# Two half-size DMAs for each streamed weight half, P.V of quad 6 inside Q of quad 7, and V's stores issued by SyncE

## The chip, the core and the metric

The kernel runs on one core of one Trainium2 chip. Its engines work side by side, each on its own stream of instructions: TensorE (PE, matmuls; PEld is its weight loads), VectorE (DVE), ScalarE (ACT), GpSimd (POOL) and SyncE (SP), which here only issues DMAs. Sixteen DMA engines move the data. The metric is the device time of one execution in microseconds; less is better.

## What is computed

Four layers in a row on a sequence of 2048 tokens of width 640: A, B, A, B, each on a layer-normed input with a residual. A is attention with a recurrent memory: the sequence is cut into 64 segments of 32 tokens, 8 memory rows stand ahead of each, and what comes out in the memory rows is the memory of the next segment. B is a dilated sliding-window attention (8 keys, 2 apart). Cut to what matters here:

```python
def _A_ref(x, mem0, Wq, Wk, Wv, Wo, seg_len):      # 32 heads of 192
    for s in range(n_seg):                         # 64 segments of 32 tokens
        h = concatenate([mem, xs])                 # 8 + 32 rows of 640
        q, k, v = h @ Wq, h @ Wk, h @ Wv           # each 640 x 6144
        p = softmax(where(mask, q @ k.T * scale, -1e9))
        o = (p @ v) @ Wo                           # 6144 x 640
        mem = o[:, :M]
        outs.append(o[:, M:])
...
x = x + _A_ref(_layernorm(x), ...)
x = x + _B_ref(_layernorm(x), ...)
x = x + _A_ref(_layernorm(x), ...)
x = x + _B_ref(_layernorm(x), ...)
```

## The kernel before

**Two lanes.** The memory makes the segments of a layer follow each other, but the second pair of layers needs only segments that the first pair has finished. So step `t` computes segment `t` of the first A layer and segment `t - 2` of the second A layer together, as two lanes of 40 rows: a matmul has 128 x 128 weights and 80 moving columns. The B layers of the segments one step back are mixed in. There are 66 steps with A and a last one with B alone; the first two and the last two have one lane (`one_lane`).

**Quads.** The 32 heads are taken four at a time, as eight quads. For quad `i` a step makes K (`a_k`), Q (`a_q`) and V (`a_v`), 30 matmuls each, in `proj`; the scores (`a_s`, eight matmuls), their exponential on ScalarE and the mask on VectorE (`a_mask`); P.V (`a_pv`, eight matmuls) and, on ScalarE behind it, the reciprocal of the sums `R` (four logarithms and an exponential); the product of P.V and `R` on VectorE (`a_norm`); and the output projection (`a_o`, 30 matmuls), which runs several quads late. P.V of quad `i - 1` stands in the iteration of quad `i`. `step` writes the order of all engines out by hand; nothing reorders it. After quad 6's iteration it goes on: K of quad 7, P.V of quad 6, Q of quad 7, output of quad 2, norm of quad 6, scores of quad 7, mask of quad 7, output of quad 3, P.V of quad 7, and then outputs of the quads that are left, the layer norm of the next step among them. `a_vt` does nothing there in a step of two lanes.

**Weights.** A's weights are 32 units (k, q, v, o by eight quads), each of two halves of 128 x 1920 bf16, 480 KB. 40 of the 64 halves stay in SBUF. The other 24 are read again in every step through a ring of four buffers (`wring`, tile `w_ring`). `prefetch` runs down a list of loads and issues those that have a free buffer; `used` is called where the last matmul that reads a half has been written and hands its buffer back, so that the DMA of the next half waits for that matmul. In `proj`, `used` for the first half is called before the 16th matmul. All weight loads are issued by SyncE, in order: what waits there holds up what stands behind it.

A streamed half lies in memory as two contiguous blocks of 128 x 960 (`PIECE`), the first for columns 0 to 959 of every partition and the second for the rest; one DMA reads both (line 264), in 256 packets of 1920 bytes. A matmul of K, Q or V reads 128 columns out of chunk `c` (384 columns each) of a half; one of the output projection, 128 columns out of row block `m` (640 columns each).

**V through memory.** For quads 2 to 7 in steps of two lanes V is transposed without TensorE: VectorE transposes 32 x 32 blocks (`v_blocks`, into `vB`), `v_send` stores them to DRAM (`v_rows`, 144 KB, 128 packets, six times a step), and `v_fetch` reads them back in another order into `Vt` (120 KB, six times a step), which P.V reads. `v_send` is issued by ScalarE's queue and `v_fetch` by SyncE's. `v_send` of quads 2 to 4 stands behind `v_fetch` of the quad before, at the end of an iteration; that of quads 5, 6 and 7 stands right behind Q of quads 3, 4 and 5.

**Completions.** Every DMA adds to one of eight completion semaphores, which the program hands out in turn over all DMAs; a DMA that takes a semaphore waits until the DMA that had it eight earlier has landed.

Of the kernel before, what the change touches and what calls it, by code (L numbers as in the profile page):

```python
# [17 lines left out]
P = 128  # L18
# [14 lines left out]
PIECE = 960  # L33
# [12 lines left out]
HALF = 1920  # L46
# [41 lines left out]
def pair_in_one(resident, kind, i):  # L88

    return all((kind, i, h) in resident for h in range(2)) and (kind, i) != ("o", NQUAD - 1)  # L90

class Kernel:
# [142 lines left out]
    def prefetch(self):  # L235

        while self.loads:
            key = self.loads[0]
            kind, i, h = key
            n = 1  # L240
            if kind == "b":
                if any(self.kept_uses[u] < 2 for u in self.under(i)):
                    return
                self.loads.pop(0)
                self.load_b_weights(i)
                continue
            if self.n_loaded < N_HALVES and key in self.kept:
                at = self.kept_at[key]
                t_ = self.wb[:, at:at + HALF]
            elif key in self.resident:  # L250
                n += pair_in_one(self.resident, kind, i)
                t_ = self.wres.tile([P, n * HALF], BF16, name="w_%s%d%d" % key)
            elif self.ring_free:
                t_ = self.wring.tile([P, HALF], BF16, name="w_ring")
                self.ring_free -= 1
            else:
                return
            del self.loads[:n]
            self.n_loaded += n
            src = self.wsrc[kind][i, P * HALF * h:P * HALF * (h + n)]  # L260
            if key in self.resident:
                self.nc.sync.dma_start(out=t_[:, 0:n * HALF], in_=src.rearrange("(p c) -> p c", p=P))
            else:
                self.nc.sync.dma_start(out=t_[:, 0:HALF].rearrange("p (a c) -> p a c", c=PIECE), in_=src.rearrange("(a p c) -> p a c", p=P, c=PIECE))
            for j in range(n):
                self.units[kind, i, h + j] = t_[:, j * HALF:(j + 1) * HALF].rearrange("p (a b) -> p a b", a=3 if kind == "o" else NC)

# [30 lines left out]

        return self.acc[int(c >= 3)], c - 3 * int(c >= 3)

    def proj(self, kind, i, t):

        nc = self.nc
        hT = self.hT
        ps = self.big(f"ps_{kind}", {"k": 0, "q": 1, "v": 2}[kind])
        w = [self.units[kind, i, h] for h in range(2)]
        mem_last = (kind, i) == (("k", 0) if self.one_lane() else ("v", VLAG))
        order = [(n, c) for c in range(NC) for n in range(6)] if mem_last else [(n, c) for n in range(6) for c in range(NC)]
        for n, c in order:
            if n == 3 and c == 0 and not mem_last:  # L310
                self.used(kind, i, (0,))
            nc.tensor.matmul(ps[:, NT * n + self.c0:NT * n + self.c1], lhsT=w[n // 3][:, c, P * (n % 3):P * (n % 3 + 1)],  # L312
                             rhs=hT[:, NT * c + self.c0:NT * c + self.c1],
                             start=(c == 0 and (n == 0 or not mem_last)), stop=(c == NC - 1), skip_group_check=mem_last)
        self.used(kind, i, (0, 1) if mem_last else (1,))
        return ps
# [8 lines left out]
        nc.scalar.copy(out=kz[0:64, :, 0, :], in_=pv[0:64, :, 1, :])  # L325
        nc.scalar.copy(out=kz[64:P, :, 1, :], in_=pv[64:P, :, 1, :])

    def a_q(self, i, t):
        ps = self.proj("q", i, t)
        qt = self.ap1.tile([P, 6, NT], BF16, name="QT")  # L330
        self.nc.vector.tensor_copy(out=self.cols(qt[:]), in_=self.cols(ps[:, 0:6 * NT].rearrange("p (a n) -> p a n", a=6)))  # L331
        self.qt = qt
# [56 lines left out]
    def v_send(self, i):  # L389

        self.v_sent[i] = self.vdp.tile([P, 3 * DH], BF16, name="v_rows")
        self.nc.scalar.dma_start(out=self.v_sent[i][:], in_=self.vB[i % 2][:])

    def v_fetch(self, i):

# [368 lines left out]
    def b_alone(self, b):  # L764
# [36 lines left out]
        scaled = lambda dst, src: nc.vector.tensor_tensor(out=dst, in0=src, in1=over_c(r), op=ALU.mult)  # L801
        qb = self.bp.tile([P, 6, NX], BF16, name="QB")[:, 0:NC, on]
        scaled(qb, proj(0, "ps_bq", 0))
        kp = proj(1, "ps_bk", 1)
        vp = proj(2, "ps_bv", 2)
        n = BG * SEG
# [59 lines left out]
    def step(self, t):  # L866
        T = self.n_seg + LAG
        self.set_lanes(t)
        b = t - 1 if t >= 1 else None
        nt = t + 1  # L870
        if t == T:
            return self.b_alone(b)
        ahead = not self.one_lane()
        if ahead:
            self.a_v(VLAG, t)
        for i in range(NQUAD - 1):
            self.a_k(i, t)
            if i >= 1:
                self.a_vt(i - 1)
            if b is not None and i == 1:  # L880
                self.b_ln_apply(b)
            if b is not None and i == 3:
                self.b_mask(b, 1)
            self.a_q(i, t)
            if ahead and 3 <= i <= 5:
                self.v_send(i + 2)
            if ahead and i in V_EARLY:
                self.a_v(V_EARLY[i], t)
            if b is not None and i == 0:
                self.bterms = self.ln_terms(self.nc.vector, self.bsums)  # L890
            if b is not None:
                self.b_first(b, i)
            if i >= 1:
                self.a_pv(i - 1)
            if b is not None and i == 6 and self.one_lane():
                self.b_ot()
            if not ahead:
                self.a_v(i, t)
            if b is not None:
                self.b_second(b, i)  # L900
            if ahead and i in V_LATE:
                self.a_v(V_LATE[i], t)
            if i >= OLAG:
                self.a_o(i - OLAG)
            if b is not None and i == 5:
                self.b_pv(1)
                self.b_norm(1)
            if i >= 1:
                self.a_norm(i - 1)
            self.a_s()  # L910
            if b is not None and i == 0:
                self.b_ln(b)
            self.a_mask()
            if ahead and V_LATE.get(i, 0) > VLAG:
                self.v_blocks(V_LATE[i])
            if ahead and i >= 1:
                self.v_fetch(i + 1)
            if ahead and i <= 2:
                self.v_send(i + 2)
            if b is not None and i == 0:  # L920
                self.b_ln_rstd()
            if b is not None and 2 <= i <= 3:
                self.b_s(2 * i - 3)
            if b is not None and i == 6:
                self.b_wo(b)
            if b in (0, LAG) and i == 6:
                self.band_block(self.maskB[0], 1, 0, int(b == LAG))
            if i == 1:
                if nt < self.n_seg:
                    self.x_load(nt)  # L930
                yseg = t - 2 - LAG
                if yseg >= 0 and yseg % 2 == 1:
                    self.y_store(yseg // 2)
        self.a_k(7, t)
        self.a_vt(6)
        if ahead:
            self.a_pv(6)
        self.a_q(7, t)
        if nt < T:
            self.ln1_sums(nt)  # L940
        if not ahead:
            self.a_pv(6)
            self.a_v(7, t)
        self.a_o(7 - OLAG)
        self.a_norm(6)
        self.a_s()
        self.a_vt(7)
        self.a_mask()
        self.a_o(8 - OLAG)
        if ahead:  # L950
            self.a_pv(7)
        self.a_o(9 - OLAG, slice(0, None if ahead else NC), ahead)
        if nt < T:
            self.ln1(nt)
        if not ahead:
            self.a_pv(7)
        if nt < T:
            self.ln1_rstd()
        self.a_norm(7)
        if not ahead:  # L960
            self.a_o(9 - OLAG, slice(NC, None))
        for i in range(10 - OLAG, 7):
            if t == 0:
                self.warm(16)
            self.a_o(i)
        if nt < T:
            self.ln1_apply(nt)
        if t == 0:
            order = [(m, c) for m in (0, 2, 1) for c in range(NC)] + [(m, c) for cs in ((0, 1, 2), (3, 4)) for m in (3, 5, 4) for c in cs]
            self.warm(8)  # L970
            self.a_o(7, slice(0, 3 * NC), False, order)
            self.warm(16)
            self.a_o(7, slice(3 * NC, None), True, order)
        else:
            self.a_o(7)
        if nt < T:
            self.mem_out(t)
        self.b_x1(t)
# [93 lines left out]
```

## Time and profile before

| | us |
|---|---|
| median of 3 runs | 3284.24 |
| the runs | 3281.96, 3284.24, 3290.99 |
| the profiled execution | 3288.64 |
| its span, first to last instruction | 3286.9 |

The profile is of one execution. Its page gives, for each engine, busy time, share of the span and number of instructions; the granted clock of TensorE (mean 0.988); the DMA queues with packets, bytes and the time that the packets took as a share of sixteen engines over the span; and the chain of work that ended last, with its shares. A view of waits lists, for each engine and line, what ended its idle time: "PE ps_q L312 <- issue: 17.8, 24, 1.9" reads as 17.8 us of TensorE's idle time ahead of line 312's matmuls into `ps_q`, in 24 pieces, the longest 1.9 us. "issue" there means that nothing which the profile shows had been waited for. A timeline lists instructions by time; start and length in us, equal ones merged with their count, and in brackets the idle time ahead and what ended it. Matmuls overlap, so the length of a merged group holds the drain of its last one. q1 is the queue of SyncE's DMAs and q10 that of ScalarE's; q8 and q14 carry instructions.

A step takes about 50 us (3286.9 us for 66 steps and a last short one).

### The profile page before, as it was taken

How to read it: one execution, taken by the hardware profiler on the slowest of the kernel's cores; microseconds unless marked ns; L12 is line 12 of the kernel's file. 1: busy time of each engine (PE TensorE's matmuls, PEld its weight loads, DVE VectorE, ACT ScalarE, POOL GpSimd, SP SyncE). 2: the span in 40 equal slices, each digit the busy share in tenths (PEclk: the TensorE clock that was granted, in tenths of full speed). 3: DMA queues.
4: the chain of work that ended last, by engine and by line, in shares of the span. 5: the costliest groups of instructions: out<-in, count | busy, mean ns of one | idle time of the engine just before them, and what ended most of it. 6: DMA issues, size and time to landing. Idle time of an engine off the chain costs nothing.

```text
span 3286.9 us, 182417 instructions
## 1 busy us (share of the span) xinstructions
PE 3060.5 (93%) x81222; PEld 2957.4 (90%) x81222; DVE 2376.9 (72%) x6010; ACT 1837.4 (56%) x5612; POOL 562.9 (17%) x1024
## 2 busy tenths in 40 slices
PE   6999999999999999999999999999999999999998
PEld 4899999999999999989999999899999999999987
DVE  3677777777777777777777777777777777777775
ACT  2456555555555556556556556556556556556554
POOL 2111111111111111111111111111112111111121
PEclk7999999999999999999999999999999999999999
DMA  9889888888888889888888888888889889888886
GB/s 378 287 278 284 285 279 275 283 274 282 277 273 277 285 262 288 278 260 283 281 267 281 283 268 285 273 273 282 273 271 283 277 281 284 282 272 286 287 276 210
DMA packets 628694, 917.18 MB, mean 279 GB/s; under 512 B 166720, under 2 KB 622912, under 8 KB 627904
## 3 DMA queue, kind: packets, MB, share of 16 engines
q1 hardware_dynamic: 560656, 845.43, 80.7%
q10 hardware_dynamic: 67248, 60.09, 5.6%
q8 instruction: 634, 10.39, 1.3%
q14 instruction: 156, 1.28, 0.1%
HBM read 847.88 MB, written 57.48 MB: 275 GB/s over the span
## 4 chain that ended last, share of the span: by engine, by line
PE 76%; ACT 7%; DMA 6%; DVE 6%; issue 5%; ACTq 0%; SPq 0%
PE ps_v L312 15%; PE ps_q L312 15%; PE ps_acc L459 14%; PE ps_k L312 13%; PE ps_o L428 4%; ACT R L432 4%; PE ps_s L407 2%; PE ps_bs L625 2%; PE ps_s L408 2%; PE ps_bk L573 1%; DMA w_ring<-in_A_Wq_dram 1%; ACT R L434 1%; PE ps_bq L573 1%; PE ps_bv L573 1%; PE ps_vt L374 1%
## 5 line engine op out<-in xcount | busy, mean ns | idle before, releaser
L432 ACT ACTIVATE R<-ps_o 64x160 f32<-64x160 f32 (+1 forms) x2112 | 622.2, 295 | 369.0 <-PE ps_o L428 242.2
L312 PEld LDWEIGHTS <-w_ring 128*128 128x128 bf16 x17550 | 717.9, 100 | 62.5 <-issue 27.3
L610 POOL TENSOR_TENSOR QX<-QB,hmask 128x448 bf16<-128x448 bf16 (+2 forms) x325 | 310.9, 965 | 1506.8 <-ACT QB L588 1085.1
L459 PE MATMUL ps_acc<-OT,w_o 128*128 128x80 bf16 (+1 forms) x9900 | 500.0, 200 | 17.9 <-issue 15.4
L324 ACT CAST KF<-ps_k 128x320 bf16<-128x320 f32 (+1 forms) x528 | 218.5, 414 | 495.6 <-PE ps_k L312 443.4
L312 PE MATMUL ps_v<-hT,w_v 128*128 128x80 bf16 (+1 forms) x10350 | 485.2, 202 | 10.4 <-issue 9.4
L312 PE MATMUL ps_q<-hT,w_q 128*128 128x80 bf16 (+1 forms) x10890 | 475.7, 201 | 19.5 <-issue 9.6
L331 DVE CAST QT<-ps_q 128x480 bf16<-128x480 f32 (+1 forms) x528 | 336.3, 637 | 165.7 <-PE ps_q L312 156.2
L312 PEld LDWEIGHTS <-w_q 128*128 128x128 bf16 x10890 | 426.9, 100 | 28.6 <-issue 20.4
L363 DVE CAST vT<-ps_v 128x480 bf16<-128x480 f32 (+1 forms) x504 | 327.9, 651 | 162.3 <-PE ps_v L312 158.4
L312 PEld LDWEIGHTS <-w_v 128*128 128x128 bf16 x10350 | 421.9, 100 | 13.1 <-issue 11.2
L459 PEld LDWEIGHTS <-w_o 128*128 128x128 bf16 x9900 | 409.4, 100 | 23.6 <-issue 20.6
L442 DVE TENSOR_TENSOR OT<-ps_o,R 128x320 bf16<-128x320 f32 (+1 forms) x528 | 252.6, 478 | 223.0 <-ACT R L434 215.4
L312 PE MATMUL ps_k<-hT,w_k 128*128 128x80 bf16 (+1 forms) x7920 | 351.6, 201 | 20.2 <-issue 16.2
L312 PE MATMUL ps_k<-hT,w_ring 128*128 128x80 bf16 (+1 forms) x7860 | 346.9, 201 | 16.2 <-issue 8.1
L459 PE MATMUL ps_acc<-OT,w_ring 128*128 128x80 bf16 (+1 forms) x5940 | 343.5, 201 | 17.0 <-issue 12.6
L410 ACT ACTIVATE E<-ps_s 80x320 bf16<-80x320 f32 (+1 forms) x528 | 220.0, 417 | 238.4 <-PE ps_s L408 231.5
L312 PEld LDWEIGHTS <-w_k 128*128 128x128 bf16 x7920 | 309.2, 100 | 27.3 <-issue 21.0
L387 DVE STREAM_TRANSPOSE vB<-vT 128x576 bf16<-128x576 bf16 x372 | 287.5, 773 | 6.4
L459 PEld LDWEIGHTS <-w_ring 128*128 128x128 bf16 x5940 | 263.1, 100 | 20.4 <-issue 14.0
L428 PE MATMUL ps_o<-E,Vt 80*128 80x80 bf16 (+1 forms) x4224 | 238.0, 199 | 39.5 <-DVE E L416 28.9
L312 PE MATMUL ps_v<-hT,w_ring 128*128 128x80 bf16 (+1 forms) x4770 | 252.0, 201 | 9.5 <-issue 6.1
(158 smaller groups left out, 4741.8 us busy)
## 6 DMA issues: line engine op xcount, KB each, us to landing
w_ring<-in_A_Wk_dram SPq DMA_DIRECT2D x524, 480.0 KB, 5.0
w_ring<-in_A_Wo_dram SPq DMA_DIRECT2D x396, 480.0 KB, 5.1
w_ring<-in_A_Wq_dram SPq DMA_DIRECT2D x328, 480.0 KB, 5.1
w_ring<-in_A_Wv_dram SPq DMA_DIRECT2D x328, 480.0 KB, 4.5
v_rows<-vB ACTq DMA_DIRECT2D x372, 144.0 KB, 4.7
Vt<-v_rows SPq DMA_DIRECT2D x372, 120.0 KB, 5.0
w_o<-in_A_Wo_dram SPq DMA_DIRECT2D x8, 480.0 KB, 10.9
w_q<-in_A_Wq_dram SPq DMA_DIRECT2D x3, 960.0 KB, 11.3
```

The source lines that it names most:

```text
L312: nc.tensor.matmul(ps[:, NT * n + self.c0:NT * n + self.c1], lhsT=w[n // 3][:, c, P * (n % 3):P * (n % 3 + 1)], rhs=hT[:, NT * c + self.c0 ...
L324: nc.scalar.copy(out=kf, in_=pv[:, :, 0:3:2, :])
L331: self.nc.vector.tensor_copy(out=self.cols(qt[:]), in_=self.cols(ps[:, 0:6 * NT].rearrange("p (a n) -> p a n", a=6)))
L363: nc.vector.tensor_copy(out=self.cols(self.vT[:, 0:6 * NT].rearrange("p (a n) -> p a n", a=6)), in_=self.cols(ps[:, 0:6 * NT].rearrange("p ...
L387: self.nc.vector.transpose(out=self.vB[i % 2][:].rearrange("p (b n c) -> p b n c", b=3, n=6), in_=src)
L410: nc.scalar.activation(out=self.cols(e[0:NT]), in_=self.cols(sv[0:NT]), func=ACT.Exp, scale=float(DH) ** -0.5)
L428: nc.tensor.matmul(self.cols(ov[:, pr, k]), lhsT=vt[0:NT, VH * pr + c0:VH * pr + c0 + P], rhs=self.cols(em[0:NT, 2 * pr + k // 2]), start= ...
L432: nc.scalar.activation(out=self.cols(r[r0:r0 + 64, :, j]), in_=self.cols(src), func=ACT.Ln)
L442: nc.vector.tensor_tensor(out=oc[:, :, 0:3:2], in0=ov[:, :, 0:4:3], in1=r, op=ALU.mult)
L459: nc.tensor.matmul(self.cols(acc[:, k]), lhsT=w[m // 3][:, m % 3, P * c:P * (c + 1)], rhs=self.cols(ot[:, m]), start=(i == 0 and m == 0 an ...
L573: nc.tensor.matmul(ps[:, NX * n + self.on.start:NX * n + self.on.stop], lhsT=self.wqkv[:, part, c, P * n:P * (n + 1)], rhs=self.h2T[:, c, ...
L610: self.nc.gpsimd.tensor_tensor(out=qx[:, 0:nh, self.on], in0=self.qb[:, c, self.on].unsqueeze(1).to_broadcast([P, nh, n]), in1=self.hmask[ ...
```

## The change

Three edits. The DMA of a streamed half becomes two, each of one contiguous block of 128 x 960 into its columns of the buffer; both are issued where the one was, one behind the other. `v_send` is issued by SyncE in place of ScalarE, at the same place of the written order. And in steps of two lanes P.V of quad 6 moves from between K and Q of quad 7 into Q of quad 7, behind the first 15 of its 30 matmuls and behind the call that hands the first half's buffer back.

```diff
@@ prefetch
             if key in self.resident:
                 self.nc.sync.dma_start(out=t_[:, 0:n * HALF], in_=src.rearrange("(p c) -> p c", p=P))
             else:
-                self.nc.sync.dma_start(out=t_[:, 0:HALF].rearrange("p (a c) -> p a c", c=PIECE), in_=src.rearrange("(a p c) -> p a c", p=P, c=PIECE))
+                for c0 in range(0, HALF, PIECE):
+                    self.nc.sync.dma_start(out=t_[:, c0:c0 + PIECE], in_=src[P * c0:P * (c0 + PIECE)].rearrange("(p c) -> p c", p=P))
@@ proj, a_q
-    def proj(self, kind, i, t):
+    def proj(self, kind, i, t, between=None):
...
             if n == 3 and c == 0 and not mem_last:
                 self.used(kind, i, (0,))
+                if between is not None:
+                    between()
...
-    def a_q(self, i, t):
-        ps = self.proj("q", i, t)
+    def a_q(self, i, t, between=None):
+        ps = self.proj("q", i, t, between)
@@ v_send
-        self.nc.scalar.dma_start(out=self.v_sent[i][:], in_=self.vB[i % 2][:])
+        self.nc.sync.dma_start(out=self.v_sent[i][:], in_=self.vB[i % 2][:])
@@ step
         self.a_k(7, t)
         self.a_vt(6)
-        if ahead:
-            self.a_pv(6)
-        self.a_q(7, t)
+        self.a_q(7, t, (lambda: self.a_pv(6)) if ahead else None)
```

## The prediction

> **What bounds the kernel now.** The page first: its row for TensorE, the chain, and the DMA queues.
>
> ```profile
> PE 3060.5 (93%) x81222; PEld 2957.4 (90%) x81222; DVE 2376.9 (72%) x6010; ACT 1837.4 (56%) x5612; POOL 562.9 (17%) x1024
> ...
> q1 hardware_dynamic: 560656, 845.43, 80.7%
> q10 hardware_dynamic: 67248, 60.09, 5.6%
> q8 instruction: 634, 10.39, 1.3%
> ...
> PE 76%; ACT 7%; DMA 6%; DVE 6%; issue 5%; ACTq 0%; SPq 0%
> ```
>
> TensorE is busy 93% of the span and carries 76% of the chain. The change removes no matmul, so all that can be won is its idle time, 3286.9 - 3060.5 = 226 us. The DMA engines stand second: their queues fill 80.7 + 5.6 + 1.3 = 87.6% of sixteen engines. Next, TensorE's own waits:
>
> ```profile
> PE ps_o L428 <- DVE E L416: 28.9, 55, 1.0
> PE ps_acc L459 <- issue: 28.0, 44, 1.8
> PE ps_k L312 <- issue: 24.3, 36, 1.5
> PE ps_q L312 <- issue: 17.8, 24, 1.9
> PE ps_v L312 <- issue: 15.5, 26, 1.6
> ...
> PE ps_o L428 <- issue: 8.5, 10, 1.9
> PE ps_q L312 <- DMA w_ring<-in_A_Wq_dram: 8.2, 11, 2.6
> PE ps_by L684 <- issue: 8.0, 6, 1.8
> ...
> PE ps_k L312 <- DMA w_ring<-in_A_Wk_dram: 7.5, 13, 1.4
> ...
> PE ps_q L312 <- ACT E L410: 5.0, 19, 0.3
> ...
> PE ps_acc L459 <- DMA w_ring<-in_A_Wo_dram: 4.1, 8, 1.8
> ...
> PE ps_v L312 <- DMA w_ring<-in_A_Wv_dram: 2.6, 4, 1.4
> ```
>
> Three kinds matter. "Issue" is the largest: the six rows give 28.0 + 24.3 + 17.8 + 15.5 + 8.5 + 8.0 = 102.1 us in 146 pieces, 0.70 us each. They hit every kind of matmul alike, so no buffer or operand is behind them. The masked exponentials of quad 6 cost 28.9 us in 55 pieces, and the streamed weights 8.2 + 7.5 + 4.1 + 2.6 = 22.4 us in 36.
>
> What "issue" is: TensorE's stream is 81222 matmuls and as many weight loads, 162444 instructions; q8 moved 634 packets, 256 instructions and 16 KB each, one per 5.2 us. A packet takes 1.3% x 16 x 3286.9 / 634 = 1.08 us on its DMA engine, one of the sixteen that work off the weights. I take the 0.70 us pieces for instruction packets that came late, about one in four (146 of 634).
>
> **The weights in two DMAs.** First the instructions. A half is 256 packets, 16 on each DMA engine; at q1's mean of 80.7% x 16 x 3286.9 / 560656 = 75.7 ns that is a share of 1.21 us, and at least that, since the mean includes small packets. If an engine turns to another queue only where a DMA's share ends, an instruction packet that meets a share waits 0.6 us on average and 1.2 at most; with shares of 8 packets 0.3 and 0.6. The trace keeps each packet's start, length and size without its engine, and no view lists them; in those records the starts of instruction packets coincide far oftener than chance with the end of a 4-byte packet, the write with which a DMA's share ends. So I take the turn to be there.
>
> The Trainium skill states that rule in "DMA: Bandwidth & Descriptors", section "Queues, rings and completion order": an engine goes round the queues that have work and drains a whole packet of some 9 to 17 descriptors from one before it switches. Its "Runtime: NRT & Kernel Launch", section "Instruction fetch mechanics", calls the cost of crossing a 16 KiB block of instructions "mostly hidden", by which the issue rows would have another cause and this term be zero; the 102.1 us in pieces of 0.70 speak against that.
>
> The gain: halving saves a packet that waited 0.3 us on average and 0.6 at most. Those that came late are the ones that waited long, so their saving lies above 0.3. V's stores leave q10 as well, so a third queue no longer takes a turn ahead of the instructions: 8 packets at 5.6% x 16 x 3286.9 / 67248 = 43.8 ns, 0.35 us, but only where a store is under way. The bounds are thus 0.3 and 0.6 + 0.35 = 0.95 us; I take 0.5, as the stores are on their way for a part of the time. With late pieces spread evenly from 0 to 1.4 us (mean 0.70, longest 1.9) a cut of d leaves (1 - d/1.4) squared: 0.41 at 0.5, 0.62 and 0.10 at the bounds. So the gain is 0.59 x 102 = 60 us, bounds 39 and 92.
>
> Now the weights themselves. SyncE issues a second DMA behind each first:
>
> ```profile
> 1603.37 1.24 PE L312 MATMUL ps_q<-hT,w_q 128*128 128x80 bf16 x30
> 1604.45 0.52 PE L459 MATMUL ps_acc<-OT,w_ring 128*128 128x80 bf16 x10
> ...
> 1600.16 0.37 SPq L264 DMA_DIRECT2D w_ring<-in_A_Wo_dram  x1
> 1600.62 0.42 SPq L398 DMA_DIRECT2D Vt<-v_rows  x1
> ...
> w_ring<-in_A_Wk_dram SPq DMA_DIRECT2D x524, 480.0 KB, 5.0
> w_ring<-in_A_Wo_dram SPq DMA_DIRECT2D x396, 480.0 KB, 5.1
> w_ring<-in_A_Wq_dram SPq DMA_DIRECT2D x328, 480.0 KB, 5.1
> w_ring<-in_A_Wv_dram SPq DMA_DIRECT2D x328, 480.0 KB, 4.5
> ```
>
> Neighbours on SyncE start 0.46 us apart (1600.16 to 1600.62), so the second piece starts that much later, 1576 times, 725 us of SyncE's 3287. That is not on the path by itself: of the 4.5 to 5.1 us from issue to landing the data of a half need 1.21 us on an engine and the rest is mostly queue, which hides the second issue, and the first piece now queues half the work. A matmul waits for the piece that it reads: three matmuls (K, Q, V) or five (output) run on the first one, and TensorE asks for the second 3 to 5 x 0.036 us later (30 matmuls of Q in 1604.45 - 1603.37 = 1.08 us). A wait that is already met costs nothing I can see. Bounds: 36 waits that end 0.46 us earlier at best (-17 us), and at worst each of them 0.46 longer and twice as many loads late (17 + 22 = +39 us). I take 0 for this, and +4 because a faster TensorE asks for the same weights sooner.
>
> The 1576 more completions, a write on each of sixteen engines, are 25216 packets; at q1's mean they would take 25216 x 75.7 ns / 16 = 119 us of each engine, 3.6% of the span. They carry 4 bytes against 1920, so I take nearly nothing on the path and keep the 3.6% for the rival.
>
> **P.V of quad 6.** The middle step of the run:
>
> ```profile
> 1601.69 0.70 PE L312 MATMUL ps_k<-hT,w_ring 128*128 128x80 bf16 x15
> 1603.09 0.45 PE L428 MATMUL ps_o<-E,Vt 80*128 80x80 bf16 x8 [0.69 <-DVE E L416]
> ...
> 1606.89 0.46 PE L428 MATMUL ps_o<-E,Vt 80*128 80x80 bf16 x8
> ...
> 1602.43 0.43 ACT L324 CAST KF<-ps_k 128x320 bf16<-128x320 f32 x1 [0.60 <-PE ps_k L312]
> 1602.76 0.28 ACT L325 CAST Kz<-ps_k 64x160 bf16<-64x160 f32 x1
> 1603.05 0.29 ACT L326 CAST Kz<-ps_k 64x160 bf16<-64x160 f32 x1
> 1603.62 1.23 ACT L432 ACTIVATE R<-ps_o 64x160 f32<-64x160 f32 x4 [0.28 <-ACT Kz L326]
> 1604.88 0.47 ACT L434 ACTIVATE R<-R 128x320 f32<-128x320 f32 x1
> ...
> 1605.39 0.49 DVE L442 TENSOR_TENSOR OT<-ps_o,R 128x320 bf16<-128x320 f32 x1
> ...
> 1606.48 0.32 DVE L416 TENSOR_TENSOR E<-E,maskA 80x320 bf16<-80x320 bf16 x1
> ```
>
> P.V waits 0.69 us for its mask; 15 matmuls of Q (0.54 us) now run in that time, which looks like a gain of 0.54 x 55 = 30 us. It is not one. From P.V of quad 6 at 1603.09 the chain goes through the four logarithms (from 1603.62) and the exponential (to 1605.35) on ScalarE, the norm on VectorE (from 1605.39) and the mask of quad 7 (1606.48 to 1606.80), and P.V of quad 7 starts at 1606.89, 0.09 us behind its mask. TensorE's own work between the two P.Vs has filled exactly these 3.80 us. P.V of quad 6 still starts at 1603.09, its mask sets that; behind it stand 0.54 us less of matmuls, so TensorE reaches P.V of quad 7 at 1606.35 and waits there for about the same 0.5 us. What is late next is the mask of quad 7, not Q. Where there was no wait ahead of P.V of quad 6, P.V starts 0.54 us later; but ScalarE casts K first (0.91 us, 1602.43 to 1603.34) and the logarithms start no later for it. So 0 us; bounds -5 (an issue stall between the two P.Vs that the new slack swallows) and +6 (11 steps of 66 x 0.54, where that cover fails).
>
> But the wait takes back a part of the first gain. It is 0.69 us in a step without a late packet, 66 x 0.69 = 46 us in all, of which 28.9 show now; 17 are hidden behind late packets ahead of it. With 59% of these gone, 10 us show again.
>
> **V's stores on SyncE.** ScalarE loses 372 issues:
>
> ```profile
> L392 ACTq DMA_DIRECT2D v_rows<-vB x372: 325/326/398, 141.1 to 3166.2; - x186
> ...
> SPq L398 <- DMA v_rows<-vB: 164.1, 117, 4.3
> ...
> SPq L264 <- DMA w_ring<-in_A_Wq_dram: 31.1, 50, 2.9
> SPq L264 <- DMA w_ring<-in_A_Wv_dram: 17.9, 31, 1.4
> ```
>
> That is 372 x 0.326 = 121 us of ScalarE, 56% busy and off the path except where it holds a bank that Q needs (5.0 us above): -3 us. On SyncE the store waits for VectorE's block transpose with the next loads behind it: at most 372 x 0.33 = 123 us of SyncE, but it stands where SyncE mostly waits for TensorE to hand back a buffer. 0 us; bounds -5 and +10.
>
> **Sum.** -60 (instructions) + 4 (weights) + 0 (P.V) + 10 (mask again) - 3 (V's stores) = -49 us against the profiled execution's 3288.64, that is 3240. That run lies 4.4 us above the median of the runs, 3284.24, so against the median 3235.
>
> **The rivals.**
>
> The instructions are not helped: the engine turns between any two packets, or what holds instruction packets back is the bytes under way, which stay the same. For it: one packet of 16 KB takes 1.08 us, longer than 8 weight packets, so it shares the engine while it runs. Against: pieces as long as 1.9 us. Then 4 - 3 + 0 = 0 +- 8: 3284 us.
>
> More is won: the late packets waited behind two shares, and the cut reaches 0.95 us. Then -92 + 4 + 14 - 3 = -77, 3207 us; with the weights' best bound 3190.
>
> Slower: SyncE becomes the bound through the eight completion semaphores. A DMA now waits for the one eight issues earlier, four halves back or fewer when stores and fetches of V lie between. SyncE already waits 31.1 + 17.9 us in 81 pieces of 0.6 us for older weight DMAs; twice the DMAs put four times as many in reach (324 x 0.6 = 194 us), each with a load of weights behind it. It decides where a load is held longer than its queue hides; if one in three reaches TensorE, 65 us, with the completions' 3.6% on top of engines 87.6% full. Less half of the instructions' gain, 65 - 30 = +35 us: 3320. Against it: 8 DMAs of 240 KB are the four buffers, and a buffer comes free only after its own DMAs landed.
>
> A rule in the same skill page, section "Rules for kernel authors", speaks for this rival: it asks for DMAs of 1 MiB or more. [...]
>
> **How the numbers follow.** My forecast: 0.62, with 3195 to 3268 as its own range (39 to 92 us of instructions and the bounds of the rest). Instructions not helped 0.18, more won 0.07, slower 0.13. The range 3190 to 3292 holds the forecast, most of the larger gain and no change. About 0.3%, 10 us, is what a measurement of this kernel tells from no change. Faster by over that: 0.62 + 0.07 and a little of the second case, 0.71; within 0.14; slower 0.15.
>
> **What would show it.** In the profile of the changed kernel: TensorE's issue waits near 42 us in place of 102; a wait of about 0.5 us at P.V of quad 7 for its mask and of 0.15 at P.V of quad 6, together some 40 us; q1 some 25 thousand packets richer, and those of V's stores in it and out of q10; waits for the ring between 5 and 60 us, and SyncE's waits for older DMAs up. If the issue rows stay near 100 us, the first term is wrong and the time is that of no change. If ring waits pass 60 us, the slower case holds.

## The result and the profile after

| | us |
|---|---|
| changed kernel, median of 4 runs | 3234.55 (3226.11 to 3237.32) |
| before, beside it, median of 4 runs | 3283.10 (3268.67 to 3290.99) |
| ratio, 95% interval | 0.9853 [0.9813, 0.9892] |
| profiled execution of the changed kernel, its span | 3236.56, 3234.5 |

Faster by 1.5%. The profiled execution fell by 3288.64 - 3236.56 = 52.1 us. Lines of the code stand 3 further down behind the edits (315 for 312, 431 for 428, 419 for 416, 265 for 264). The page of the changed kernel, its rows for the engines, the DMA queues and the chain:

```profile
PE 3061.1 (95%) x81222; PEld 2953.9 (91%) x81222; DVE 2375.0 (73%) x6010; ACT 1838.6 (57%) x5612; POOL 562.7 (17%) x1024
...
q1 hardware_dynamic: 639504, 900.41, 88.9%
q8 instruction: 634, 10.39, 1.4%
q10 hardware_dynamic: 13680, 5.21, 0.7%
...
PE 65%; DMA 24%; ACT 4%; DVE 3%; issue 2%; SPq 2%; ACTq 0%
```

TensorE's work is the same (3061.1 against 3060.5 us), so the whole gain is idle time: 3234.5 - 3061.1 = 173 us where there were 226. (In the rows of the queues the second figure is megabytes; a packet there is one contiguous piece of a transfer.) In the chain "issue" fell from 5% to 2% and DMA rose from 6% to 24%: the path now runs through transfers. What TensorE waits for (us in total, times, longest):

```profile
PE ps_q L315 <- DMA w_ring<-in_A_Wq_dram: 37.1, 68, 1.9
PE ps_acc L462 <- DMA w_ring<-in_A_Wo_dram: 16.2, 41, 1.8
PE ps_o L431 <- DVE E L419: 16.2, 45, 0.6
PE ps_o L431 <- DMA Vt<-v_rows: 16.1, 27, 1.2
PE ps_k L315 <- DMA w_ring<-in_A_Wk_dram: 12.5, 27, 1.7
PE ps_v L315 <- DMA w_ring<-in_A_Wv_dram: 12.1, 21, 1.7
...
PE ps_acc L462 <- issue: 5.0, 8, 1.3
PE ps_q L315 <- issue: 4.1, 9, 1.0
...
PE ps_k L315 <- issue: 2.8, 8, 0.8
PE ps_v L315 <- issue: 2.4, 6, 0.9
```

Before, the order was the reverse: issue rows of 15 to 28 us, rows of the ring of 3 to 8. The loads, from the page (count, KB each, median us from issue to landing):

```profile
w_ring<-in_A_Wk_dram SPq DMA_DIRECT2D x1048, 240.0 KB, 4.5
w_ring<-in_A_Wo_dram SPq DMA_DIRECT2D x792, 240.0 KB, 5.1
w_ring<-in_A_Wq_dram SPq DMA_DIRECT2D x656, 240.0 KB, 4.6
w_ring<-in_A_Wv_dram SPq DMA_DIRECT2D x656, 240.0 KB, 4.0
v_rows<-vB SPq DMA_DIRECT2D x372, 144.0 KB, 4.6
```

Half the bytes take about as long as the whole did (4.0 to 5.1 us against 4.5 to 5.1). SyncE's own waits for DMAs:

```profile
SPq L401 <- DMA v_rows<-vB: 66.9, 94, 2.6
SPq L265 <- DMA w_ring<-in_A_Wo_dram: 41.4, 131, 1.4
SPq L265 <- DMA w_ring<-in_A_Wq_dram: 39.0, 100, 1.2
```

`v_fetch` waits for V's store 67 us instead of 164; the loads wait longer for older loads. The way from P.V of quad 6 to P.V of quad 7 in one step of the changed kernel, rows of several engines (start and length in us):

```profile
1283.62 0.32 DVE L419 TENSOR_TENSOR E<-E,maskA 80x320 bf16<-80x320 bf16 x1
...
1284.00 0.45 PE L431 MATMUL ps_o<-E,Vt 80*128 80x80 bf16 x8
...
1284.28 0.70 PE L315 MATMUL ps_q<-hT,w_q 128*128 128x80 bf16 x15
...
1284.53 1.23 ACT L435 ACTIVATE R<-ps_o 64x160 f32<-64x160 f32 x4 [0.19 <-ACT Kz L329]
...
1285.79 0.47 ACT L437 ACTIVATE R<-R 128x320 f32<-128x320 f32 x1
...
1286.29 0.49 DVE L445 TENSOR_TENSOR OT<-ps_o,R 128x320 bf16<-128x320 f32 x1 [0.61 <-ACT R L437]
...
1287.38 0.32 DVE L419 TENSOR_TENSOR E<-E,maskA 80x320 bf16<-80x320 bf16 x1
...
1287.75 0.34 PE L431 MATMUL ps_o<-E,Vt 80*128 80x80 bf16 x5 [0.33 <-DVE E L419]
```

P.V of quad 6 does not wait in this step; 3.75 us later P.V of quad 7 does, 0.33 us, behind its mask. Medians over all steps follow below.

### The profile page after: what moved, and what is told of

It is laid out like the page before. It is cut to its first block, busy times and chain, and to the rows that moved or that the text cites. A ratio compares the mean times of both kernels' runs of the same rounds, so it can differ in the third digit from the quotient of the medians.

```text
span 3234.5 us, 184090 instructions
## 1 busy us (share of the span) xinstructions
PE 3061.1 (95%) x81222; PEld 2953.9 (91%) x81222; DVE 2375.0 (73%) x6010; ACT 1838.6 (57%) x5612; POOL 562.7 (17%) x1024
## 3 DMA queue, kind: packets, MB, share of 16 engines
q1 hardware_dynamic: 639504, 900.41, 88.9%
q10 hardware_dynamic: 13680, 5.21, 0.7%
## 4 chain that ended last, share of the span: by engine, by line
PE 65%; DMA 24%; ACT 4%; DVE 3%; issue 2%; SPq 2%; ACTq 0%
PE ps_v L315 14%; PE ps_k L315 12%; PE ps_acc L462 11%; PE ps_q L315 11%; DMA Vt<-v_rows 8%; DMA w_ring<-in_A_Wq_dram 6%; DMA w_ring<-in_A_Wo_dram 4%; PE ps_o L431 3%; DMA w_ring<-in_A_Wk_dram 2%; ACT R L435 2%; PE ps_bs L628 2%; PE ps_s L410 2%; SPq L265 2%; PE ps_bk L576 1%; PE ps_bq L576 1%
## 5 line engine op out<-in xcount | busy, mean ns | idle before, releaser
L315 PE MATMUL ps_q<-hT,w_q 128*128 128x80 bf16 (+1 forms) x10890 | 483.8, 201 | 10.4 <-DMA w_q<-in_A_Wq_dram 5.5
L462 PE MATMUL ps_acc<-OT,w_ring 128*128 128x80 bf16 (+1 forms) x5940 | 352.1, 201 | 18.9 <-DMA w_ring<-in_A_Wo_dram 16.2
L462 PEld LDWEIGHTS <-w_ring 128*128 128x128 bf16 x5940 | 266.5, 100 | 28.9 <-DMA w_ring<-in_A_Wo_dram 23.5
L315 PE MATMUL ps_q<-hT,w_ring 128*128 128x80 bf16 (+1 forms) x4920 | 242.1, 201 | 39.2 <-DMA w_ring<-in_A_Wq_dram 37.1
L431 PE MATMUL ps_o<-E,Vt 80*128 80x80 bf16 (+1 forms) x4224 | 237.3, 199 | 36.8 <-DVE E L419 16.2
```

Source lines behind the costliest of these rows:

```text
L431: nc.tensor.matmul(self.cols(ov[:, pr, k]), lhsT=vt[0:NT, VH * pr + c0:VH * pr + c0 + P], rhs=self.cols(em[0:NT, 2 * pr + k // 2]), start= ...
L462: nc.tensor.matmul(self.cols(acc[:, k]), lhsT=w[m // 3][:, m % 3, P * c:P * (c + 1)], rhs=self.cols(ot[:, m]), start=(i == 0 and m == 0 an ...
```

## The experiments

The first table is worked out: TensorE's idle time by cause, each the sum of all rows of that kernel's view of waits (us, in brackets times). "Ring" is waiting for a streamed weight, "Vt" for V on its way back from DRAM, "mask" P.V's wait for VectorE's mask. "Held by ScalarE" is Q waiting for the exponential of the scores (ACT E) and the B layers' rows that wait for VectorE's `On`.

| kernel | issue | ring | Vt | mask | held by ScalarE | all |
|---|---|---|---|---|---|---|
| before | 116.2 (170) | 22.4 (36) | 0.3 | 28.9 (55) | 5.0 + 10.8 | 216.4 |
| changed | 20.8 (46) | 79.3 (159) | 16.1 (27) | 16.2 (45) | 0 + 0.6 | 160.5 |
| e1_two_dmas | 14.5 (29) | 30.1 (62) | 26.1 (24) | 27.9 (43) | 30.5 + 23.3 | 185.9 |
| e2_v_on_sync | 106.3 (143) | 46.9 (71) | 1.9 | 27.5 (54) | 0 + 1.4 | 215.6 |
| e3_pv_alone | 110.8 (156) | 26.0 (42) | 1.6 | 20.2 (56) | 3.8 + 9.9 | 201.2 |
| e4_rows_3840 | 131.5 (180) | 20.7 (31) | 0 | 30.2 (57) | 4.0 + 11.3 | 225.5 |
| e5_changed_again | 16.6 (31) | 70.8 (147) | 14.9 (28) | 19.6 (53) | 0 + 0.8 | 154.1 |
| e6_v_on_scalar | 12.2 (27) | 29.3 (55) | 14.7 (23) | 17.6 (51) | 31.1 + 24.9 | 158.1 |
| e7_no_pv_move | 20.4 (38) | 72.8 (150) | 32.2 (40) | 13.6 (23) | 0 + 1.2 | 172.0 |
| e8_quarter_rows | 0.9 (1) | 381.0 (645) | 184.9 (118) | 1.2 | 0 + 0.4 | 608.4 |
| e9_thirds | 2.5 (6) | 217.0 (416) | 100.7 (92) | 9.0 | 0 + 0.4 | 364.6 |
| e10_partition_halves | 298.4 (300) | 294.6 (315) | 36.6 | 2.8 | 0 + 0.6 | 689.8 |
| e11_uneven_cut | 23.2 (48) | 64.1 (100) | 16.9 (31) | 17.9 (51) | 0 + 0.4 | 152.9 |
| e12_store6_later | 16.9 (32) | 73.9 (153) | 15.7 (30) | 17.0 (49) | 0 + 0.8 | 157.8 |

The times, each beside runs of before on the same chip:

| kernel | us | ratio to before, 95% interval |
|---|---|---|
| e1_two_dmas | 3248.59 | 0.9907 [0.9878, 0.9937] |
| e2_v_on_sync | 3273.33 | 0.9989 [0.9972, 1.0005] |
| e3_pv_alone | 3270.56 | 0.9966 [0.9948, 0.9985] |
| e4_rows_3840 | 3285.56 | 1.0021 [1.0002, 1.0040] |
| e5_changed_again | 3222.42 | 0.9820 [0.9797, 0.9844] |
| e6_v_on_scalar | 3222.83 | 0.9835 [0.9810, 0.9860] |
| e7_no_pv_move | 3237.77 | 0.9859 [0.9832, 0.9886] |
| e8_quarter_rows | 4072.93 | 1.2415 [1.2388, 1.2443] |
| e9_thirds | 3512.23 | 1.0707 [1.0669, 1.0745] |
| e10_partition_halves | 3896.55 | 1.1853 [1.1822, 1.1884] |
| e11_uneven_cut | 3237.13 | 0.9856 [0.9839, 0.9873] |
| e12_store6_later | 3234.91 | 0.9848 [0.9826, 0.9871] |

### Each edit alone

**The two DMAs.** Before, with the loop of `prefetch` alone:

```diff
-                self.nc.sync.dma_start(out=t_[:, 0:HALF].rearrange("p (a c) -> p a c", c=PIECE), in_=src.rearrange("(a p c) -> p a c", p=P, c=PIECE))
+                for c0 in range(0, HALF, PIECE):
+                    self.nc.sync.dma_start(out=t_[:, c0:c0 + PIECE], in_=src[P * c0:P * (c0 + PIECE)].rearrange("(p c) -> p c", p=P))
```

> The kernel before with the first edit alone: each streamed half by two DMAs. My theory (an instruction packet waits until the DMA share that its engine works on has ended, and a share is now half as long): TensorE's issue waits fall from 102 us in the six largest rows to between 25 and 50, waits for the ring rise from 22 to 50 to 80, and the time is 40 us below the kernel before, 3243 (3225 to 3262). Rival (the whole gain needs V's stores off ScalarE's queue, so that one queue less takes turns): issue waits stay above 80 us and the time is within 12 us of the kernel before.

Faster by 0.9%. The number and size of the data packets, the order and the queues are those of before; the cut is new, with 1576 more issues and completions, and with it issue falls from 116 to 14.5 us (13.9 in the six largest rows, where 25 to 50 were expected). TensorE's rows in e1, the largest and the largest of issue:

```profile
PE ps_q L313 <- ACT E L411: 30.5, 50, 1.5
PE ps_o L429 <- DVE E L417: 27.9, 43, 0.8
PE ps_o L429 <- DMA Vt<-v_rows: 26.1, 24, 3.5
PE ps_bo L652 <- DVE On L667: 22.9, 48, 0.5
...
PE ps_acc L460 <- issue: 4.5, 10, 0.9
```

That is 102 us of idle time gone and 72 come back, and not where the forecast looked: the ring rose by 8 where 28 to 58 were expected, Vt by 26, and what ScalarE holds by 38.

**V's stores.** Before, with SyncE as the issuer of `v_send` alone:

```diff
-        self.nc.scalar.dma_start(out=self.v_sent[i][:], in_=self.vB[i % 2][:])
+        self.nc.sync.dma_start(out=self.v_sent[i][:], in_=self.vB[i % 2][:])
```

> The kernel before with the third edit alone: V's stores issued by SyncE. My theory: the shares of the weights are as long as before, so the issue waits fall a little only, to 85 to 100 us, SyncE's waits ahead of the fetches of V change little, and the time is 0 to 15 us below the kernel before. Rival (one queue less is what counts): issue waits below 60 us and a gain of 30 us or more.

No change that can be told from none. ScalarE's 16 us at Q and at `On` go, and the ring takes 24 more, mostly at Q:

```profile
PE ps_acc L459 <- issue: 27.2, 31, 2.6
PE ps_k L312 <- issue: 26.0, 36, 2.4
PE ps_q L312 <- DMA w_ring<-in_A_Wq_dram: 25.7, 38, 3.9
```

Issue stays at 106 us, 91 of them in the six largest rows, as expected (85 to 100): V's bytes on a third queue were not what held the instructions back.

**P.V.** Before, with P.V of quad 6 in the middle of Q alone (`between`, as in the change):

```diff
-        if ahead:
-            self.a_pv(6)
-        self.a_q(7, t)
+        self.a_q(7, t, (lambda: self.a_pv(6)) if ahead else None)
```

> The kernel before with the second edit alone: P.V of quad 6 in the middle of Q of quad 7. My theory: the wait for the mask moves from P.V of quad 6 to P.V of quad 7, 0.5 us each, and TensorE's waits for the masked exponentials stay within 8 us of 28.9; the time is within 8 us of the kernel before. Rival (the 15 matmuls fill the wait): these waits fall below 12 us and the time by 15 to 30 us.

Faster by 0.34% (0.15 to 0.52), some 11 us, where a time within 8 us of before was expected. Medians over the 62 steps of two lanes, in us, worked out from the trace's instructions:

```
                   wait at   P.V 6 behind   P.V 6 to   wait at
                   P.V 6     its mask's end   P.V 7    P.V 7
before             0.42      0.15           3.81       0.00
e3_pv_alone        0.00      0.05           3.79       0.34
e1_two_dmas        0.70      0.15           3.80       0.00
changed            0.06      0.40           3.79       0.33
```

The 3.8 us from one P.V to the next hold in every kernel, as forecast: the wait moved to quad 7. But P.V of quad 6 starts 0.10 us sooner behind its mask, 62 x 0.10 = 6 us. In before, a separate wait instruction stands ahead of its weight loads (all instructions of P.V's line on the loading side, with durations in ns, minimum/median/maximum):

```profile
L428 PEld LDWEIGHTS <-Vt x4224: 95/98/152, 17.7 to 3271.3; 80*128 80x128 bf16 x192
L428 PEldq EVENT_SEMAPHORE  x62: 51/51/51, 173.9 to 3175.0; - x62
```

One for each of the 62 steps; in e3 the line has no such instruction. That it costs the 0.10 us is inferred from this. Issue, 5 us lower in e3, may be the rest.

### What holds the instructions back

**Half the packets, one DMA.** Before, with a streamed half as one contiguous block, 128 packets of 3840 bytes:

```diff
-                self.nc.sync.dma_start(out=t_[:, 0:HALF].rearrange("p (a c) -> p a c", c=PIECE), in_=src.rearrange("(a p c) -> p a c", p=P, c=PIECE))
+                self.nc.sync.dma_start(out=t_[:, 0:HALF], in_=src.rearrange("(p c) -> p c", p=P))
```

> The kernel before with the streamed halves laid out like the resident ones: still one DMA for a half, but of 128 packets of 3840 bytes in place of 256 of 1920. A DMA's share on an engine is half as many packets with the same bytes. My theory (the time of a share counts): issue waits stay near 100 us (85 to 120) and the time within 12 us of the kernel before. Rival (the number of packets ahead counts, or an engine turns between any two packets): with 8 packets as in the changed kernel issue waits fall below 50 us; with turns between any two packets, now twice as long, they rise above 140.

```profile
PE ps_k L312 <- issue: 33.2, 44, 2.8
PE ps_o L428 <- DVE E L416: 30.2, 57, 1.0
PE ps_acc L459 <- issue: 26.3, 31, 2.3
PE ps_q L312 <- issue: 21.9, 36, 1.2
```

A DMA's share on an engine has 8 packets, as in the changed kernel, but issue is 131.5 us (112 in the six largest rows, within the 85 to 120 expected) and the time that of before. So it is not the number of packets; with e1, where packets and bytes are the same, what counts is into how many DMAs the bytes are cut.

**What the waits are.** The instructions and packet records of the same traces, worked out, tie the issue waits to the instruction packets. Counted along TensorE's stream, two instructions to a matmul, all 170 issue waits of before stand at instruction 192 or 193 of a block of 256, and so do all 46 of the changed kernel and all 180 of e4; its other waits are spread over the block. Ahead of every one of the 170 the last 16 KB packet that landed is the one with the block's own number, and 93% of them end 1.2 to 1.6 us behind its landing, where 8% would by chance. So TensorE waits there for its next 256 instructions. The time from the first matmul of a block to the start of the packet for the next block, over all blocks (e11 and e9 follow below):

```
                     mean us   exceeded by one in ten
before                 2.09      3.37
e2_v_on_sync           2.06      3.27
e4_rows_3840           2.16      3.42
e11_uneven_cut         1.79      2.69
e1_two_dmas            1.56      2.43
changed, e5          1.64, 1.49  2.54, 2.37
e9_thirds              1.19      1.94
```

The two DMAs bring a packet forward by 0.53 us in the mean and by 0.93 us among the late ones (e1). Where it starts fits the turn at the end of a share: 68% of the instruction packets of before, and 60% in the changed kernel, start within 5 ns of the end of a 4-byte packet, against 11% and 18% by chance.

**An uneven cut.** The changed kernel, with three quarters of a half in the first DMA:

```diff
+CUTS = ((0, 1440), (1440, 1920))
...
-                for c0 in range(0, HALF, PIECE):
-                    self.nc.sync.dma_start(out=t_[:, c0:c0 + PIECE], in_=src[P * c0:P * (c0 + PIECE)].rearrange("(p c) -> p c", p=P))
+                for c0, c1 in CUTS:
+                    self.nc.sync.dma_start(out=t_[:, c0:c1], in_=src[P * c0:P * c1].rearrange("(p c) -> p c", p=P))
```

> The changed kernel with its two DMAs cut at 3 to 1: 128 packets of 2880 bytes and 128 of 960, so as many DMAs, completions and issues as in the changed kernel. My theory (an instruction packet waits for the rest of the share that it meets, and longer shares are met more often): the mean rest is (9 + 1) / 16 = 0.62 of that of one DMA where two equal ones give 0.50, and the longest is 0.75 in place of 0.50; issue waits lie between those of one DMA and of two equal ones, 30 to 60 us, and the time is 5 to 30 us above the changed kernel. Rival (the number of DMAs counts, not the length of a share): issue waits 12 to 27 us as in the changed kernel.

The longest share is half as long again, and issue is 23.2 us against 20.8 and 16.6 in the two profiles of the changed kernel; the time is the same. So the 30 to 60 us expected by the length of the share did not come, and the rival's 12 to 27 us did: the length of the longest share does not set these waits. The delay of a packet, 1.79 us in the mean (table above), does lie between those of one DMA and of two equal ones, but by no more than two profiles of one kernel differ (1.64 and 1.49). Shorter shares, a second end to every half, or the half microsecond between the two issues: which of them helps was not settled.

**By halves of the partitions.** The changed kernel, with the cut between partitions 63 and 64 instead of between columns:

```diff
-                for c0 in range(0, HALF, PIECE):
-                    self.nc.sync.dma_start(out=t_[:, c0:c0 + PIECE], in_=src[P * c0:P * (c0 + PIECE)].rearrange("(p c) -> p c", p=P))
+                for p0 in range(0, P, P // 2):
+                    self.nc.sync.dma_start(out=t_[p0:p0 + P // 2, 0:HALF], in_=src[HALF * p0:HALF * (p0 + P // 2)].rearrange("(p c) -> p c", p=P // 2))
```

> The changed kernel with its two DMAs cut by partitions: each of 64 partitions, in 64 packets of 3840 bytes. A DMA's share on an engine is 4 packets with the same bytes as 8 of 1920. My theory (the time of a share sets the instructions' wait): issue waits between 12 and 30 us; a matmul now needs both pieces at once, but the packets cost the DMA engines less time (78.4% against 80.7% with one DMA), so ring waits stay between 55 and 95 us and the time within 12 us of the changed kernel. Rival (what counts is 128 packets over all engines, or 64 partitions do not reach all sixteen engines): issue waits above 60 us, or a time 30 us or more above the changed kernel.

Slower by 18.5% with the same bytes, and issue 298 us where 12 to 30 were expected. This says nothing of the cut in two, since the weights' transfers became slower. The queue of SyncE in e10:

```profile
q1 hardware_dynamic: 437264, 900.41, 95.4%
```

and in e4, which has the same packets of 3840 bytes on all partitions:

```profile
q1 hardware_dynamic: 358416, 845.43, 78.4%
```

The mean packet takes 95.4% x 16 x 3897.2 / 437264 = 136 ns against 78.4% x 16 x 3296.6 / 358416 = 115 ns, though e10's q1 also has V's small ones. By the packet records, one of 3840 bytes takes 253 ns in the median against 149 (249 against 184 in the mean). All sixteen engines are at work, since q1 alone fills 95.4% of them. With the engines full, instructions and weights are late alike (298 and 295 us).

### How far the cut goes

The changed kernel with `PIECE = 640`, three DMAs to a half, and with `PIECE = 480`, four:

```diff
-PIECE = 960
+PIECE = 640
```

> The changed kernel with three DMAs for each streamed half, of 128 packets of 1280 bytes. My theory (what ended the gain with four DMAs is SyncE's time to issue, 0.59 us for each in a row there, not the completion semaphores): 5521 DMAs of 0.55 to 0.59 us are 3040 to 3260 us of SyncE, about the whole span, so the time is 3260 to 3400 us, SyncE's waits for compute fall from 1105 to between 350 and 700 us, and issue waits of TensorE stay below 10 us. Rival (completion semaphores): SyncE's waits for older weight DMAs rise above 250 us.

> The changed kernel with four DMAs for each streamed half, of 128 packets of 960 bytes: shares of the same 8 packets and half the bytes. My theory: issue waits fall further, below 12 us; but eight completion semaphores now reach back two halves only, so SyncE's waits for older weight DMAs rise from 119 us to 400 or more, ring waits from 79 to over 150, and the time is above the changed kernel by 20 us or more. Rival (completions cost nothing): ring waits within 30 us of 79 and a time at or below the changed kernel.

Issue goes on falling (2.5 and 0.9 us), and the time rises by 7% and 24%; the thirds, 3512 us, are slower than the 3260 to 3400 expected. The chain of e8:

```profile
PE 35%; DMA 33%; SPq 26%; issue 4%; DVE 1%; ACT 0%; ACTq 0%; DVEq 0%
```

and SyncE's timeline in e8, hardly a gap in it:

```profile
2000.03 4.75 SPq L265 DMA_DIRECT2D w_ring<-in_A_Wk_dram  x8
2004.88 0.38 SPq L395 DMA_DIRECT2D v_rows<-vB  x1
2005.36 3.05 SPq L265 DMA_DIRECT2D w_ring<-in_A_Wq_dram  x4
2008.50 1.80 SPq L265 DMA_DIRECT2D w_ring<-in_A_Wv_dram  x4
```

SyncE, with the sums of all rows of its waits taken from the span, per DMA (streamed pieces and V's 744):

```
changed   (3234.5 - 1375.8) / (3152 + 744) = 0.48 us, waits 43% of the span
thirds    (3505.3 -  674.5) / (4728 + 744) = 0.52 us, waits 19%
quarters  (4072.5 -  412.9) / (6304 + 744) = 0.52 us, waits 10%
```

Half a microsecond per DMA: with quarters SyncE is at it for 90% of the span, and a freed buffer waits for its DMA. The wait for older weight DMAs, the mechanism that was named for the slower side, is not it: 160 us (381 times) in the changed kernel, 115 in the thirds and 30 in the quarters.

### The edits beside each other

**The changed kernel once more**, as the base for the next two.

> The changed kernel itself, beside the next three on one chip: 0.9853 of the kernel before (0.981 to 0.989), issue waits near 21 us, ring waits near 79 us.

On this chip it came out at 0.9820 (0.9797 to 0.9844), with 16.6 us of issue and 70.8 of the ring. The sums of two profiles of one kernel thus differ by up to 9 us.

**V's stores back on ScalarE**, the other two edits kept:

```diff
-        self.nc.sync.dma_start(out=self.v_sent[i][:], in_=self.vB[i % 2][:])
+        self.nc.scalar.dma_start(out=self.v_sent[i][:], in_=self.vB[i % 2][:])
```

> The changed kernel with V's stores back on ScalarE's queue. My theory (with two DMAs for a half, the store of quad 6 takes a completion semaphore whose last owner is a weight DMA still under way, and holds ScalarE's queue): Q's waits for ScalarE's exponentials, gone in the changed kernel, are 20 to 40 us, ring waits 25 to 45 us in place of 79, and the time is 5 to 15 us above the changed kernel. Rival (the store's queue makes no difference once the shares are short): within 4 us of it, with no waits for the exponentials at Q.

The same time (3222.8 against 3222.4 us), by other waits: 56 us at Q and `On`, held by ScalarE, against 0.8, and 29.3 of the ring against 70.8. TensorE's rows in e6:

```profile
PE ps_q L315 <- ACT E L413: 31.1, 47, 1.2
PE ps_bo L654 <- DVE On L669: 24.5, 52, 0.5
...
PE ps_k L315 <- DMA w_ring<-in_A_Wk_dram: 9.3, 24, 1.5
...
PE ps_q L315 <- DMA w_ring<-in_A_Wq_dram: 7.0, 12, 1.6
```

The 5 to 15 us expected did not come, and the reason named for ScalarE's hold is not what the trace shows. ScalarE's own waits in e6:

```profile
ACT R L435 <- DVE vB L390: 72.9, 50, 1.5
...
ACT KF L327 <- DMA w_ring<-in_A_Wk_dram: 0.5, 1, 0.5
```

Only the store of V needs `vB`, VectorE's transposed blocks: ScalarE waits for them ahead of the store, with the rest of its work behind, and hardly for a weight DMA. (The row is 38.4 us before, 79.8 in e1, and absent where SyncE issues the store.)

**P.V back ahead of Q**, the other two kept:

```diff
-        self.a_q(7, t, (lambda: self.a_pv(6)) if ahead else None)
+        if ahead:
+            self.a_pv(6)
+        self.a_q(7, t)
```

> The changed kernel with P.V of quad 6 back between K and Q: the first and third edits alone. My theory: as in the kernel with the second edit alone, the move is worth about 9 us because P.V starts 0.05 instead of 0.15 us behind its mask; waits for the masked exponentials rise from 16 us to 35 to 55, almost all at P.V of quad 6, and the time is 5 to 15 us above the changed kernel. Rival (worth nothing beside the other two): within 4 us of it.

15 us slower than the changed kernel (3237.8 against 3222.4; 0.9859 against 0.9820, intervals of 0.3% and 0.2% that just overlap). The time is as expected, its reason is not: the waits for the mask were to rise to 35 to 55 us and are 13.6. The Vt row doubles instead, 32.2 against 14.9 us, 30.9 of it at P.V of quad 6, where V now comes later than the mask: in the middle of Q, P.V of quad 6 more often finds its V there.

**V's store of quad 6 later**, behind V of the next quad in the iteration of quad 4, to bring the weights of Q forward:

```diff
-            if ahead and 3 <= i <= 5:
+            if ahead and 3 <= i <= 5 and i != 4:
                 self.v_send(i + 2)
...
                 self.a_v(V_LATE[i], t)
+            if ahead and i == 4:
+                self.v_send(6)
```

> The changed kernel with the store of V of quad 6 issued behind V of quad 7, some 2 us later in SyncE's order, so that the weights of Q of quad 5 go ahead of it. My theory (SyncE's issue time is what makes these weights late, not the engines): ring waits fall from 71 to 79 us to between 45 and 65, waits for V's fetches stay below 30 us, and the time is 3 to 15 us below the changed kernel. Rival (these weights are late for another reason): ring waits within 8 us of 71 to 79 and a time within 4 us of the changed kernel.

No change, as the rival had it (0.9848 against 0.9853 and 0.9820): the ring keeps 73.9 us, 39.5 of them at Q (38.7 in e5). That store's place is not what makes the weights of Q late; what does stays open.

## Why the prediction was right

The time, 3234.55 us, is the forecast, 3235. The mechanism of the first term held, but several terms were off and cancelled. Term by term, against the waits before and after (table above):

**Instructions, -60.** Right in kind, too small. The six largest issue rows were to fall from 102.1 to 42 us; they fell to 18.2 (-84 us), and all rows from 116.2 to 20.8 (-95 us). By the forecast's own formula, 18.2 / 102.1 = 0.18 left means a cut of 0.81 us, not 0.5. The bound of 0.95 contained it, but only by V's stores; e1 leaves 13.9 of 102.1 with those still on ScalarE, a cut of 0.88 us by the formula and 0.93 measured among the late packets, so the cut in two is worth more than the 0.6 us allowed for it. One part of this is the packet's price: the mean of q1, 75.7 ns, holds the small packets too, and one of 1920 bytes takes 95 ns in the mean, so a share of 16 is 1.5 us and not 1.21. That the cut is what helps is shown by e1, e2 and e4 together. The rival that nothing helps is out: an engine that turned between any two packets would treat e1 as before. That the gain comes by the shorter share, and not by the number of ends or the pause between them, is not shown (e11).

The Trainium skill's "DMA: Bandwidth & Descriptors", section "Queues, rings and completion order", with its turn at the end of a packet of descriptors, fits these runs; that such a packet is a DMA's whole share is the forecast's own step. "Mostly hidden" in "Runtime: NRT & Kernel Launch", section "Instruction fetch mechanics", holds by count, since 464 of 634 blocks before and 588 in the changed kernel came without such a wait, but it does not make the term zero: the 170 blocks that came late cost 116 us before, and the 29 in e1 14.5.

**Weights, +4.** The term that was furthest off: the ring rose by 57 us (22.4 to 79.3), above its bound of 39, and Vt by 16, which was not in the sum. The test "over 60 us, and the slower case holds" was wrong: waits passed 60 and the kernel was faster. Most of it is not the second DMA (e1: ring +8) but V's stores on SyncE (e5 against e6: 41 more); that the place of the store among the loads is what does it is not shown (e12 moved one and changed nothing).

**V's stores, -3.** Its two sides were far larger than 5.0 us and 0 and nearly cancel: what ScalarE holds fell by 15 us here, and by 55 against e6, and the ring rose by 41. The edit's worth: 0.1% alone, which cannot be told from nothing (e2), within 0.15% on top of both others (e5, e6), 0.5% on top of the two DMAs alone (e7 against e1, on two chips, with intervals of 0.3% each).

**P.V, 0, and +10 for the mask.** The chain of 3.8 us and the wait at quad 7 were right (0.33 us against 0.5 forecast). Missed were the 0.10 us at quad 6, so that nothing was left there instead of 0.15, and the cover for a late V. The mask's waits fell from 28.9 to 16.2 us instead of rising by 10. The 0.69 us of one step that the forecast took for all 66 is not typical of before, whose median is 0.42 over 62 steps; in e1, without the late packets, it is 0.70, so the wait did come back there, about half of it for V and not for the mask (23 and 27 us). In the changed kernel the move took it away. The edit is worth 0.34% alone and 0.4% on top of the others.

Against the sum: issue 35 us better than forecast, the mask 23, ScalarE 12; the ring and Vt 57 + 16 - 4 = 69 worse. 35 + 23 + 12 = 70 against 69 is luck in the sizes. **What the page was to show:** q1 gained 639504 - 560656 = 78848 packets, of which 67248 - 13680 = 53568 left q10; the other 25280 are the completions (25216 forecast).

**The slower rival** exists, further out and by another mechanism: three DMAs to a half are slower than before, because issuing costs SyncE half a microsecond each (clear for the quarters, inferred for the thirds, where SyncE still waited for 19% of the span), not because of the eight semaphores. The rule of the Trainium skill that spoke for it ("DMA: Bandwidth & Descriptors", section "Rules for kernel authors", 1 MiB or more) is about bandwidth, and the engines did pay for the cut (q1 82.7% full in e1 against 80.7%), but from 480 to 240 KB the kernel got 0.9% faster (e1); at 160 and 120 KB the rule points the right way, though SyncE's issuing had grown there as well.

## What to carry to other kernels

When an engine with a long instruction stream shows waits for nothing in particular, spread over all its lines, look whether they come at fixed steps of its stream, and at how the DMAs beside it are cut: the same bytes in two DMAs instead of one took 100 us of such waits away. Count the issues first: at 0.5 us each, the queue that issues them must keep room to wait for buffers (43% of the span here; at 19% the kernel was already slower than before). And a gain of 95 us in one kind of wait brought 52: what was behind comes forward, here weights and V, so look at which transfer is next before the sum is made.

## What the runs showed that was not expected

Loads into 64 partitions cost more than the same bytes into 128: 253 ns against 149 in the median for a packet of 3840 bytes, and 18.5% of the kernel's time, with two DMAs to the two halves of one buffer behind each other.

TensorE's busy time grew in the kernels in which it waited long. The granted clock was 0.991 in the changed kernel, 0.982 in the thirds and 0.951 in the quarters, and the busy time of the same 81222 matmuls 3061.1, 3128.2 and 3387.3 us, so of the 4072.5 - 3234.5 = 838 us that the quarters lost, 326 are in TensorE's busy time. The clock explains less than half of these (0.991 / 0.951 is 4.2%, 129 us); the rest stays open. Nor does the clock follow the waits alone: e10 waited longer than the quarters (690 us against 608) at a higher clock (0.961) and was busy for 3195.0 us.
